# Crossbar transposes for five chunks, a seven-product form of the second MLP product for four chunks, and two groups of zero products, in an attention and Fourier-mixing kernel

## The chip, the cores and the metric

One core of a Trainium2 chip runs the program. The metric is the device time in microseconds of one execution; less is better. The profile is of one execution, and its span runs from the first to the last instruction.

TensorE (PE) multiplies a stationary block with a moving one and writes to PSUM; VectorE (DVE), ScalarE (ACT) and GpSimd (POOL) work on elements; SyncE (SP) issues most transfers. Each engine takes its instructions in the order of its own queue and waits for others by semaphores.

## The reference

```python
# attention with a bias by distance; a key is kept if it is among the first 8,
# or at most 95 places before the query
scores = scale * q @ k.T + bias            # B=4, H=8, S=768, D=64
x = softmax(where(keep, scores, -1e9)) @ v # then heads side by side: B x 768 x 512

# Fourier mixing and a two-layer MLP
mixed = real(fft(fft(x, axis=1), axis=2))
u = x + mixed
un = (u - mean(u)) / sqrt(var(u) + 1e-6)
out = u + relu(un @ w_ch1) @ w_ch2         # w_ch1: 512 x 2048, w_ch2: 2048 x 512
```

## The kernel before

The work falls into four batches. For each one the kernel makes scores, exponentials and the product with V (unit `av`), normalises (`norm`, L699 and L700) into `x`, writes it to DRAM and reads it back in another order of rows (`bounce`), and folds it by additions and subtractions on VectorE (`fold_3`, `fold_s`, `fold_d`). Two stages of small products then make the Fourier transform: `y_unit` (py, L881) and `u_unit` (pu, L961); `mirror` copies reversed blocks on POOL between them.

The MLP takes each batch in three chunks of 256 rows, so there are chunks 0 to 11; chunk 3b + pr belongs to batch b. A chunk consists of two blocks t = 0, 1 of 128 rows. `u_unit` adds the input to the transform (L980), takes the mean away and scales (`un`, L995 on ACT, L997 on DVE). `nt_unit` transposes `un` by eight products with the identity (ptu, L1025) and copies the result out of PSUM to `unT` (L1033 on ACT or L1035 on DVE). The squares for the variance (L1004) overwrite `un`, so they come after the transposes.

The first MLP product of a chunk, `ph_unit` (ph, L1053), has eight units of eight products that are 256 wide; ACT (L1059) or DVE (L1060) applies the maximum with zero and writes `hT`, of which there are three buffers. The second, `pg_unit` (pg, L1076), has four units of four products for each t, 512 wide, all summed in one PSUM bank; L1085 multiplies with the reciprocal deviation and adds to `u`, and a store to the output follows (L1090). The rings `ph` and `pg` have two banks each; `u` has four buffers, `un` and `unT` two.

No loop sets the order. A class `Plan` holds a modelled clock for each engine and, while the program is written, always emits next what can start first in that model. There are four streams for PE: MIX and ATT, in which one of the first ten units can be chosen, and PH and PG, which stay in order. Work for the other engines is announced with `pl.later(ways, needs, after, outs, uses, ...)`: engine and modelled time, what must be there, what it makes, which buffers it frees. Among such operations that could start at the same modelled time, the lower `rank` goes first, then the one that was ready first, then the one announced first. The modelled times decide the order of the queues only; on the chip the semaphores decide.

Of batches 2 and 3 the q and k blocks are already transposed by transfers (`trans_dma`, L494). `expst` holds the exponentials, `mk` the masks that batches 2 and 3 multiply with (L587), `EG` the exponentials of the first eight keys; `EG` is zero at the start, and twelve products with it (L1116) open PE's queue. `v_place` (pvp, L427) puts V of batches 0 and 1 in place by products.

Of the kernel before, what the change touches and what calls it, by code (L numbers as in the profile page):

```python
# [12 lines left out]
ALU = mybir.AluOpType  # L13
# [142 lines left out]
def mm_us(n, k=1):  # L156
    return k * max(n / 2400.0 + 0.0025, 0.029)
# [6 lines left out]
def dve(n):  # L164
    return 0.085 + n / 960.0


def dve2(n):
    return 0.075 + n / 1920.0
# [7 lines left out]
def kernel(  # L177
# [106 lines left out]
    def free(tag, i):  # L284
        i -= NBUF[tag]
        return [("free", tag, i)] if i >= 0 else []

    def buf(tag, i, shape, dtype, users):
        pl.users(("free", tag, i), users)
        return wk.tile(shape, dtype, tag=tag, name=f"{tag}_{i}", bufs=NBUF[tag])  # L290
# [16 lines left out]
    kG = [kon.tile([P, HP, 32], FP16, tag=f"kG{i}", name=f"kG{i}") for i in range(2)]  # L307
    vG = [kon.tile([P, H, 66], FP16, tag=f"vG{i}", name=f"vG{i}") for i in range(2)]

    MIX, ATT, PH, PG = [], [], [], []  # L310
    V = nc.vector
    VT = nc.vector.tensor_tensor
# [105 lines left out]
    def v_place(b, hp):  # L418
        n = HP * b + hp

        def run(start, ring):
            pv = bank(ring, f"pvp_{n}")
            for x in range(NP):
                for a in range(2):
                    for t in range(2):
                        r = slice(64 * a, 64 * a + 64)
                        nc.tensor.matmul(pv[64 * t:64 * t + 64, a, x * P:(x + 1) * P], idn[r, r],  # L427
                                         V0[n][r, x, t].rearrange("p h d -> p (h d)"), start=True, stop=True,
                                         tile_position=(64 * a, 64 * t))
            e = pl.pe(mm_us(P, 12), start)  # L430
            pl.used(("free", "er", n), e)
            done = []

            def freed(t):
                done.append(t)
                if len(done) == 2:
                    pl.rings[ring].append(max(done))
                    for x in CD(b, ring):
                        pl.used(x, max(done))
            for a in range(2):  # L440
                dst = v16[b][:, a::2, 2 * hp:2 * hp + 2, 0:Dh]
                src = pv[:, a, 0:3 * P].rearrange("p (n h d) -> p n h d", h=2, d=Dh)
                ways = [("DVE", dve(384), lambda dst=dst, src=src: V.tensor_copy(dst, src)),
                        ("ACT", act(384), lambda dst=dst, src=src: A(dst, src, AF.Copy))]
                pl.later(ways[a:a + 1],
                         [], e, [("v", b, hp, a)], rank=RA(b), then=freed)
        ATT.append(([("vc", n), ("c", "id")], BANKS(b), run))
# [169 lines left out]
                         e, [("vG", b, half)], (CD(b, ring) if last else ()), ring=ring if last else None, rank=RA(b))  # L617
        ATT.append((VN(b, [2 * half + i for half in halves for i in range(2)]) + [("one", 0)], BANKS(b), run))

    EG = kon.tile([P, 512], FP16, tag="eg", name="eg")  # L620

    def glob(b, halves):

# [326 lines left out]
    def u_unit(b, pr):  # L950
# [62 lines left out]
            pl.later([("POOL", 1.0, rstd)], [("ss", c, 0), ("ss", c, 1)], 0.0, [("rstd", c)], rank=2)  # L1013
        MIX.append((needs + [("c", "t2")], BANKS(b), run))

    def nt_unit(b, pr):
        c = NP * b + pr

        def run(start, ring):
            pt = bank("xx", f"ptu_{c}", FP16)  # L1020
# [22 lines left out]
    def ph_unit(c, jp):  # L1043
        needs = [("unT", c), ("w1", jp // 2)] + (free("hT", 5 + c) if jp == 0 else []) + [("CD",)]

        def run(start, ring):
            if jp == 0:
                HT[c] = buf("hT", 5 + c, [P, NJ, CH], FP16, 2)
            ph = bank("ph", f"ph_{c}_{jp}")
            for a in range(2):  # L1050
                jb = 2 * jp + a
# [14 lines left out]
    def pg_unit(c, t, part):  # L1066
# [4 lines left out]
        def run(start, ring):  # L1071
# [18 lines left out]
                nc.sync.dma_start(out[b].rearrange("(m r) d -> m r d", r=6)[:, rs, :], UT[c][:, t, :])  # L1090
            pl.later([("SP", 0.45, st)], [("ob", i)], 0.0, [], [("free", "u", 2 * HP + c)], lat=1.6, dma=0.7)
        PG.append((needs, ("pg",) if part == 0 else None, run))


    def dma_const(dst, src, us, tok, needs=()):
# [2 lines left out]
    with tc.manual_schedule():  # L1098
# [151 lines left out]
        for c in range(NP * B):  # L1250
            for jp in range(NJ // 2):
                ph_unit(c, jp)
            for t in range(2):
                for part in range(4):
                    pg_unit(c, t, part)
        pl.run([(MIX, True), (ATT, True), (PH, False), (PG, False)])


# [33 lines left out]
```

## Time and profile before

| | us |
|---|---|
| median of 14 runs | 278.48 |
| lowest, highest | 277.04, 280.16 |
| profiled execution | 279.05 |
| its span | 277.3 |
| busy in the span: PE, weight loads, DVE, ACT, POOL | 260.0, 174.3, 157.6, 147.3, 59.7 |

The clock of PE was granted in full except in the slices around 50 us. What is busy where, in 40 equal slices (tenths of a slice):

```profile
PE   8698899589789999999999999999999999999994
PEld 3344548549667864677586566777866677767441
DVE  4565854974785515665378968666896662111121
ACT  1485585584766643797772138888242256434000
POOL 1445195730002502413110031401001320100000
PEclk9999999899999999999999999999999999999999
```

Each slice is 6.9 us long. A busy share is no limit by itself; the last instructions and what they waited for are read from the chain and the timeline, below.

Where the chunks stand on PE's timeline, counting 64 products of ph and 32 of pg for each:

| chunk | transposes (ptu) | first product (ph) begins |
|---|---|---|
| 7 | 172.43 | 183.0 |
| 8 | 176.07 | 195.7 |
| 9 | 221.47 | 224.1 |
| 10 | 223.65 | 234.1 |
| 11 | 230.19 | 246.3 |

The last product of chunk 11's ph ends at 256; after it the pg products of chunks 9 (second half), 10 and 11 follow.

### The profile page before, as it was taken

The numbers are of one execution on the slowest core, as the hardware profiler recorded it, in microseconds if no ns is written. First come the engines' busy times: TensorE is split into PE (matmuls) and PEld (weight loads), VectorE is DVE, ScalarE is ACT, GpSimd is POOL, SyncE is SP. The second block draws the span as 40 slices with busy tenths as digits, with TensorE's granted clock in tenths as the row PEclk, the third lists the DMA queues.
The fourth block names the chain that finished last, engine by engine and source line by source line (L and its number), as shares of the span: only waits on it lengthen the run. The fifth ranks groups of instructions, "written<-read, shape, count | busy, mean of one in ns | idle before, by whom it ended". The sixth has DMA issues, their size and how long they took to land.

```text
span 277.3 us, 6029 instructions
## 1 busy us (share of the span) xinstructions
PE 260.0 (94%) x2460; PEld 174.3 (63%) x2460; DVE 157.6 (57%) x323; ACT 147.3 (53%) x255; POOL 59.7 (22%) x127
## 2 busy tenths in 40 slices
PE   8698899589789999999999999999999999999994
PEld 3344548549667864677586566777866677767441
DVE  4565854974785515665378968666896662111121
ACT  1485585584766643797772138888242256434000
POOL 1445195730002502413110031401001320100000
PEclk9999999899999999999999999999999999999999
DMA  7999999995935597986987896300163020110122
GB/s 206 291 292 286 356 279 230 205 203 105 256 118 168 117 160 167 219 152 132 216 163 166 155 297 130 69 2 0 40 157 150 0 78 1 40 38 27 51 76 76
DMA packets 70301, 40.69 MB, mean 147 GB/s; under 512 B 27394, under 2 KB 66306, under 8 KB 70274
## 3 DMA queue, kind: packets, MB, share of 16 engines
q1 hardware_dynamic: 61474, 29.83, 44.2%
q0 software_dynamic: 4224, 4.19, 9.3%
q10 hardware_dynamic: 4576, 6.29, 8.3%
q8 instruction: 19, 0.31, 0.5%
q14 instruction: 8, 0.07, 0.1%
HBM read 31.92 MB, written 9.44 MB: 149 GB/s over the span
## 4 chain that ended last, share of the span: by engine, by line
PE 77%; DVE 7%; SPq 5%; ACT 3%; DMA 3%; issue 2%; POOL 1%; ACTq 1%; DVEq 0%; POOLq 0%
PE pg L1076 29%; PE ph L1053 29%; PE py L881 5%; SPq L365 4%; PE pav L680 3%; PE sc L552 3%; PE pu L961 3%; DMA w<-in_q_dram 3%; PE ptu L1025 2%; ACT ex L575 1%; PE pav L669 1%; DVE sm L984 1%; DVE qkT L521 1%; POOL ww L929 1%; SPq L1096 1%
## 5 line engine op out<-in xcount | busy, mean ns | idle before, releaser
L1053 PE MATMUL ph<-unT,w 128*128 128x256 f16 x768 | 93.8, 273 | 2.2 <-DVE hT L1060 2.2
L1076 PE MATMUL pg<-w,hT 128*128 128x512 f16 x384 | 89.9, 379 | 0.0
L1053 PEld LDWEIGHTS <-w 128*128 128x128 f16 x768 | 72.6, 98 | 18.4 <-issue 6.1
L1059 ACT ACTIVATE hT<-ph 128x512 f16<-128x512 f32 x73 | 43.6, 597 | 47.6 <-PE ph L1053 46.5
L1076 PEld LDWEIGHTS <-hT 128*128 128x128 f16 x384 | 36.9, 98 | 36.3 <-issue 0.4
L1085 DVE SCALAR_TENSOR_TENSOR u<-pg,sm,u 128x512 f32<-128x512 f32 x24 | 18.0, 749 | 53.6 <-PE pg L1076 53.3
L575 ACT ACTIVATE ex<-sc 128x992 f16<-128x992 f32 (+2 forms) x24 | 20.9, 927 | 13.9 <-PE sc L552 10.1
L1060 DVE TENSOR_SCALAR hT<-ph 128x512 f16<-128x512 f32 x23 | 15.9, 690 | 11.7 <-PE ph L1053 11.6
L572 ACT ACTIVATE er<-sc 128x992 f16<-128x992 f32 (+2 forms) x24 | 21.5, 923 | 1.1 <-PE sc L552 1.1
L369 ACT ACTIVATE qk<-qs 128x384 f16<-128x384 f32 (+1 forms) x31 | 14.5, 528 | 9.9 <-DMA qkT<-qk 7.6
L1011 POOL TENSOR_SCALAR sm<-sm 128x2 f32<-128x2 f32 x12 | 3.1, 262 | 71.6 <-ACT un L1004 71.4
L980 DVE SCALAR_TENSOR_TENSOR u<-pu,xr 128x512 f32<-128x512 f32 x24 | 15.6, 687 | 4.5 <-PE pu L961 3.9
L680 PE MATMUL pav<-v,ex 128*128 128x65 f16 x352 | 16.7, 195 | 1.3 <-ACT ex L575 1.3
L552 PE MATMUL sc<-qkT 64*128 64x256 f16 (+1 forms) x192 | 16.9, 264 | 0.6 <-DVE qkT L521 0.6
L929 POOL COPY ww<-zy 128x512 f16<-128x512 f16 x16 | 9.3, 611 | 37.9 <-PE py L881 37.9
L587 DVE TENSOR_TENSOR ex<-er,mk 128x992 f16<-128x992 f16 (+2 forms) x24 | 14.8, 626 | 4.6 <-ACT er L572 4.4
L680 PEld LDWEIGHTS <-ex 128*128 128x128 f16 x352 | 15.5, 99 | 2.6 <-issue 1.9
L995 ACT ACTIVATE un<-u,sm 128x512 f16<-128x512 f32 x12 | 8.5, 716 | 15.9 <-DVE sm L984 12.9
L1004 ACT ACTIVATE un<-un 128x512 f16<-128x512 f16 x24 | 14.8, 620 | 1.6 <-PE ptu L1025 1.6
L552 PEld LDWEIGHTS <-qkT 64*128 64x128 f16 x192 | 5.9, 94 | 14.7 <-issue 12.2
L898 DVE CAST zy<-py 128x512 f16<-128x512 f32 (+1 forms) x9 | 8.3, 926 | 10.5 <-ACT zy L896 6.4
L896 ACT ACTIVATE zy<-py 128x512 f16<-128x512 f32 (+1 forms) x10 | 8.1, 809 | 11.7 <-PE py L881 11.6
(103 smaller groups left out, 307.4 us busy)
## 6 DMA issues: line engine op xcount, KB each, us to landing
out_dram<-u SPq DMA_DIRECT2D x24, 256.0 KB, 2.3
w<-in_moe_w_ch_dram POOLq DMA_DIRECT2D x8, 512.0 KB, 12.6
qs<-in_q_dram SPq DMA_DIRECT2D x9, 384.0 KB, 5.1
qs<-in_k_dram SPq DMA_DIRECT2D x9, 384.0 KB, 5.9
u<-in_v_dram SPq DMA_DIRECT2D x8, 384.0 KB, 7.3
xr<-xd ACTq DMA_DIRECT2D x4, 768.0 KB, 4.6
qs<-in_v_dram SPq DMA_DIRECT2D x16, 192.0 KB, 4.2
w<-in_q_dram SPq DMA_DIRECT2D x4, 384.0 KB, 6.8
```

Of the source, the lines that this page charges most:

```text
L552: nc.tensor.matmul(pa[:, s, c0:c0 + cw], TT[n][lo:lo + 64, 1, i * P:(i + 1) * P], TT[n][lo:lo + 64, 0, i * P:i * P + cw], start=(b > 1), s ...
L572: A(mine(), cut(pa), AF.Exp, 0.0, 0.125)
L575: A(cut(expst[hp][:, :, g * 512:g * 512 + (384 if g == 2 else 512)]), cut(pa), AF.Exp, 0.0, 0.125)
L587: VT(o, mine(), m, op=ALU.mult)
L680: nc.tensor.matmul(po[:, jj, hh * 65:(hh + 1) * 65], lhsT, v16[b % 2][:, i, h, 0:65], start=(jp == 0 and a == 0), stop=(a == len(ops) - 1) ...
L980: V.scalar_tensor_tensor(u[:, a].rearrange("p (n r) -> p n r", r=4), pu[:, a].rearrange("p (r n) -> p n r", r=4), 1.0, XR[b][:, rr].rearra ...
L1004: A(x, x, AF.Square, accum_out=MV[c][:, a, 2:3])
L1053: nc.tensor.matmul(ph[:, a * CH:(a + 1) * CH], W1[0][:, d, jb * P:(jb + 1) * P], UNT[c][:, d, :], start=(d == 0), stop=(d == ND - 1))
L1059: pl.later([("ACT", act(512), lambda: A(dst, ph, AF.Relu)), ("DVE", dve(512), lambda: V.tensor_scalar_max(dst, ph, 0.0))], [], e, [("h", c ...
L1060: ("DVE", dve(512), lambda: V.tensor_scalar_max(dst, ph, 0.0))],
L1076: nc.tensor.matmul(pg, HT[c][:, jb, t * P:(t + 1) * P], W2[0][:, jb, :], start=(jb == 0), stop=(jb == NJ - 1))
L1085: V.scalar_tensor_tensor(UT[c][:, t, :], pg, MV[c][:, t, 3:4], UT[c][:, t, :], op0=ALU.mult, op1=ALU.add)
```

## The change

It has three parts.

- Chunks 7 to 11: `nt_dma` takes the place of the PE transposes. Two transfers on SP's queue, one for each t, write `unT` directly.
- Chunks 8 to 11: the second product is made from seven block products. `hT` is a matrix of 2 x 2 blocks (t by halves of the 2048), `w_ch2` one of 2 x 2 blocks (halves of the 2048 by halves of the 512 columns). `w2_sums` makes four sums of blocks of `w_ch2`, once, and keeps them in `expst`; `s_sums` makes four sums of blocks of `hT` for each chunk, three in `mk`, one in place. `pg_units` multiplies: seven products of eight matmuls, 256 wide, in five units (`p1`, `p45`, `p6`, `p32`, `p7`) with two PSUM banks, A and D. After each unit one addition to `u` follows, five in all. Bank A is summed into further: the left block of u(0) takes it after `p1`, the right block after `p6`, and both blocks of u(1) take it after `p7`; bank D goes to both blocks of u(1) after `p45`, and, partly summed further, to both of u(0) after `p32`.
- In `v_place` of batch 0 ten products of zeros stand before the second placement (n = 1) and fourteen after the first (n = 0). They write a part of the bank that nothing reads. `EG` is allocated earlier for them.

```diff
--- before.py
+++ after.py
@@ -307,6 +307,7 @@
     kG = [kon.tile([P, HP, 32], FP16, tag=f"kG{i}", name=f"kG{i}") for i in range(2)]
     vG = [kon.tile([P, H, 66], FP16, tag=f"vG{i}", name=f"vG{i}") for i in range(2)]
 
+    EG = kon.tile([P, 512], FP16, tag="eg", name="eg")
     MIX, ATT, PH, PG = [], [], [], []
     V = nc.vector
     VT = nc.vector.tensor_tensor
@@ -420,6 +421,9 @@
 
         def run(start, ring):
             pv = bank(ring, f"pvp_{n}")
+            idle = lambda k: [nc.tensor.matmul(pv[:, 1, 3 * P:4 * P], EG[:, 0:P], EG[:, 0:P], start=True, stop=True) for _ in range(k)]
+            if n == 1:
+                idle(10)
             for x in range(NP):
                 for a in range(2):
                     for t in range(2):
@@ -427,6 +431,8 @@
                         nc.tensor.matmul(pv[64 * t:64 * t + 64, a, x * P:(x + 1) * P], idn[r, r],
                                          V0[n][r, x, t].rearrange("p h d -> p (h d)"), start=True, stop=True,
                                          tile_position=(64 * a, 64 * t))
+            if n == 0:
+                idle(14)
             e = pl.pe(mm_us(P, 12), start)
             pl.used(("free", "er", n), e)
             done = []
@@ -617,7 +623,6 @@
                          e, [("vG", b, half)], (CD(b, ring) if last else ()), ring=ring if last else None, rank=RA(b))
         ATT.append((VN(b, [2 * half + i for half in halves for i in range(2)]) + [("one", 0)], BANKS(b), run))
 
-    EG = kon.tile([P, 512], FP16, tag="eg", name="eg")
 
     def glob(b, halves):
 
@@ -1013,8 +1018,19 @@
             pl.later([("POOL", 1.0, rstd)], [("ss", c, 0), ("ss", c, 1)], 0.0, [("rstd", c)], rank=2)
         MIX.append((needs + [("c", "t2")], BANKS(b), run))
 
+    def nt_dma(c):
+        for a in range(2):
+            def xb(a=a):
+                if a == 0:
+                    UNT[c] = buf("unT", c, [P, ND, CH], FP16, 1)
+                nc.sync.dma_start_transpose(UNT[c][:, :, a * P:(a + 1) * P], T[("un", c)][:, a])
+            pl.later([("SP", 1.3, xb)], [("un", c, a)] + (free("unT", c) if a == 0 else [("nx", c, 0)]), 0.0, [("nx", c, a)], lat=0.0, dma=0.01)
+        pl.later([("SP", 0.0, lambda: None)], [("nx", c, 1)], 0.0, [("unT", c)], [("free", "un", c)], lat=2.2, dma=0.3)
+
     def nt_unit(b, pr):
         c = NP * b + pr
+        if c >= 7:
+            return nt_dma(c)
 
         def run(start, ring):
             pt = bank("xx", f"ptu_{c}", FP16)
@@ -1045,7 +1061,7 @@
 
         def run(start, ring):
             if jp == 0:
-                HT[c] = buf("hT", 5 + c, [P, NJ, CH], FP16, 2)
+                HT[c] = buf("hT", 5 + c, [P, NJ, CH], FP16, 2 if c < CS else 1)
             ph = bank("ph", f"ph_{c}_{jp}")
             for a in range(2):
                 jb = 2 * jp + a
@@ -1090,6 +1106,146 @@
                 nc.sync.dma_start(out[b].rearrange("(m r) d -> m r d", r=6)[:, rs, :], UT[c][:, t, :])
             pl.later([("SP", 0.45, st)], [("ob", i)], 0.0, [], [("free", "u", 2 * HP + c)], lat=1.6, dma=0.7)
         PG.append((needs, ("pg",) if part == 0 else None, run))
+
+
+    NK = NJ // 2
+    HC = Dm // 2
+    CS = 8
+    SX = {}
+
+    def W2T(i):
+        return expst[i].rearrange("p s n -> p (s n)")[:, 0:NK * HC].rearrange("p (k n) -> p k n", n=HC)
+
+    def w2_sums(i):
+
+        def run():
+            k0 = slice(4 * i, 4 * i + 4)
+            k1 = slice(NK + 4 * i, NK + 4 * i + 4)
+            w = W2[0]
+            b11, b12 = w[:, k0, 0:HC], w[:, k0, HC:Dm]
+            b21, b22 = w[:, k1, 0:HC], w[:, k1, HC:Dm]
+            VT(W2T(1)[:, k0], b22, b12, op=ALU.subtract)
+            VT(W2T(3)[:, k0], b12, b11, op=ALU.subtract)
+            VT(W2T(0)[:, k0], b22, W2T(3)[:, k0], op=ALU.subtract)
+            VT(W2T(2)[:, k0], b21, W2T(0)[:, k0], op=ALU.subtract)
+        pl.later([("DVE", 4 * dve2(1024), run)], [("avdone", B - 1), ("w2", 3)] + [("ex", B - 1, hp, g) for hp in range(HP) for g in range(3)], 0.0, [("w2t", i)], rank=2)
+
+    def s_sums(c):
+        hs = [("h", c, jp) for jp in range(NJ // 2)]
+
+        def block(t, half):
+            return HT[c][:, half * NK:(half + 1) * NK, t * P:(t + 1) * P]
+
+        def new(i):
+            k = 3 * (c - CS) + i
+            pl.users(("free", "sx", k), 2 if i < 2 else 1)
+            SX[c, i] = mk.rearrange("p h n -> p (h n)")[:, (k % 4) * NK * P:(k % 4 + 1) * NK * P].rearrange("p (k n) -> p k n", n=P)
+            return SX[c, i]
+
+        def s1():
+            VT(new(0), block(1, 0), block(1, 1), op=ALU.add)
+
+        def s3():
+            VT(block(1, 0), block(0, 0), block(1, 0), op=ALU.subtract)
+
+        def s2():
+            VT(new(1), SX[c, 0], block(0, 0), op=ALU.subtract)
+
+        def s4():
+            VT(new(2), block(0, 1), SX[c, 1], op=ALU.subtract)
+        us = dve2(NK * P)
+
+        def sfree(i):
+            k = 3 * (c - CS) + i - 4
+            return [("free", "sx", k)] if k >= 0 else []
+        pl.later([("DVE", us, s1)], hs + sfree(0), 0.0, [("s", c, 1)], rank=1)
+        pl.later([("DVE", us, s2)], [("s", c, 1)] + sfree(1), 0.0, [("s", c, 2)], [("free", "sx", 3 * (c - CS))], rank=1)
+        pl.later([("DVE", us, s4)], [("s", c, 2)] + sfree(2), 0.0, [("s", c, 4)], [("free", "sx", 3 * (c - CS) + 1)], rank=1)
+        pl.later([("DVE", us, s3)], [("s", c, 1)], 0.0, [("s", c, 3)], rank=1)
+
+    def pg_units(c):
+        b, pr = divmod(c, NP)
+        rs = PAIRS[pr]
+        t1s, t2s, t3s, t4s = 0, 0, 1, 2
+
+        def prod(o, lhs, rhs, first, last=True):
+            for j in range(NK):
+                nc.tensor.matmul(o, lhs(j), rhs(j), start=(first and j == 0), stop=(j == NK - 1), skip_group_check=True)
+
+        def a(t, half):
+            return lambda j: HT[c][:, half * NK + j, t * P:(t + 1) * P]
+
+        def sx(i):
+            return lambda j: SX[c, i][:, j, :]
+
+        def bw(half, col):
+            return lambda j: W2[0][:, half * NK + j, col * HC:(col + 1) * HC]
+
+        def tw(i):
+            return lambda j: W2T(i)[:, j, :]
+        u = lambda t: UT[c][:, t, :]
+        r = lambda t: MV[c][:, t, 3:4]
+        one_us = mm_us(HC, NK)
+
+        def stt(o, x, t, acc):
+            V.scalar_tensor_tensor(o, x, r(t), acc, op0=ALU.mult, op1=ALU.add)
+
+        def p1(start, ring):
+            A_ = GP[c, "A"] = bank("pg", f"pgA_{c}")
+            prod(A_[:, 0:HC], a(0, 0), bw(0, 0), True)
+            e = pl.pe(one_us, start)
+            pl.later([("DVE", dve(HC), lambda: stt(u(0)[:, 0:HC], A_[:, 0:HC], 0, u(0)[:, 0:HC]))],
+                     [("rstd", c)], e, [("ra", c, 0)], rank=0)
+
+        def p45(start, ring):
+            D_ = GP[c, "D"] = bank("pg", f"pgD_{c}")
+            prod(D_[:, 0:HC], a(1, 1), tw(2), True)
+            prod(D_[:, HC:Dm], sx(0), tw(3), True)
+            e = pl.pe(2 * one_us, start)
+            pl.used(("free", "sx", 3 * (c - CS)), e)
+            pl.later([("DVE", dve(Dm), lambda: stt(u(1), D_, 1, u(1)))],
+                     [("rstd", c)], e, [("rd", c, 0)], rank=0)
+
+        def p6(start, ring):
+            A_ = GP[c, "A"]
+            prod(A_[:, 0:HC], sx(1), tw(0), False)
+            e = pl.pe(one_us, start)
+            pl.used(("free", "sx", 3 * (c - CS) + 1), e)
+            pl.later([("DVE", dve(HC), lambda: stt(u(0)[:, HC:Dm], A_[:, 0:HC], 0, u(0)[:, HC:Dm]))],
+                     [], e, [("ra", c, 1)], rank=0)
+
+        def p32(start, ring):
+            D_ = GP[c, "D"]
+            prod(D_[:, HC:Dm], sx(2), bw(1, 1), False)
+            prod(D_[:, 0:HC], a(0, 1), bw(1, 0), True)
+            e = pl.pe(2 * one_us, start)
+            pl.used(("free", "sx", 3 * (c - CS) + 2), e)
+            pl.later([("DVE", dve(Dm), lambda: stt(u(0), D_, 0, u(0)))],
+                     [("ra", c, 1)], e, [("ob", c, 0)], ring="pg", rank=0)
+
+        def p7(start, ring):
+            A_ = GP[c, "A"]
+            prod(A_[:, 0:HC], a(1, 0), tw(1), False)
+            e = pl.pe(one_us, start)
+            pl.used(("free", "hT", 5 + c), e)
+
+            def last():
+                o = u(1).rearrange("p (x n) -> p x n", x=2)
+                stt(o, A_[:, 0:HC].unsqueeze(1).to_broadcast([P, 2, HC]), 1, o)
+            pl.later([("DVE", dve(Dm), last)], [("rd", c, 0)], e, [("ob", c, 1)], ring="pg", rank=0)
+
+        h0 = [("h", c, jp) for jp in range(4)]
+        h1 = [("h", c, jp) for jp in range(4, 8)]
+        ws = [("w2t", 0), ("w2t", 1)]
+        PG.append((h0 + ws, ("pg",), p1))
+        PG.append((h1 + [("s", c, 1)], ("pg",), p45))
+        PG.append(([("s", c, 2), ("ra", c, 0)], None, p6))
+        PG.append(([("s", c, 4), ("rd", c, 0)], None, p32))
+        PG.append(([("s", c, 3), ("ra", c, 1)], None, p7))
+        for t in range(2):
+            def st(t=t):
+                nc.sync.dma_start(out[b].rearrange("(m r) d -> m r d", r=6)[:, rs[t], :], u(t))
+            pl.later([("SP", 0.45, st)], [("ob", c, t)], 0.0, [], [("free", "u", 2 * HP + c)], lat=1.6, dma=0.7)
 
 
     def dma_const(dst, src, us, tok, needs=()):
@@ -1250,9 +1406,15 @@
         for c in range(NP * B):
             for jp in range(NJ // 2):
                 ph_unit(c, jp)
+            if c >= CS:
+                s_sums(c)
+                pg_units(c)
+                continue
             for t in range(2):
                 for part in range(4):
                     pg_unit(c, t, part)
+        for i in range(2):
+            w2_sums(i)
         pl.run([(MIX, True), (ATT, True), (PH, False), (PG, False)])
 
 
```

## The prediction

> **What bounds the kernel now.** I read the page first (span, slices, chain, groups), then the busy time in stages, then the timeline of TensorE and VectorE around the places that the change touches. The profiled run took 279.05 us; its span is 277.3 us, so 1.75 us lie around it. The median of the 14 runs is 278.48 us, 0.57 below the profiled one. I sum against 279.05 and take 0.57 off at the end.
>
> The chain of waits says what carries the end:
>
> ```profile
> PE 77%; DVE 7%; SPq 5%; ACT 3%; DMA 3%; issue 2%; POOL 1%; ACTq 1%; DVEq 0%; POOLq 0%
> ```
>
> The reader is to see that TensorE (PE) alone is three quarters of it. By stage:
>
> ```profile
> 98.00:133.00 35.00, 35.00 (x286) 23.18 (x285) 17.73 (x34) 22.39 (x44) 8.15 (x20) 1.00 0.87 165
> 133.00:182.00 49.00, 49.00 (x459) 31.87 (x456) 35.60 (x72) 28.30 (x51) 8.27 (x21) 1.00 0.75 166
> 182.00:199.00 17.00, 17.00 (x222) 13.21 (x219) 12.16 (x24) 12.10 (x20) 0.88 (x2) 1.00 0.05 17
> 199.00:214.00 15.00, 15.00 (x107) 10.22 (x105) 12.50 (x25) 5.45 (x8) 0.10 (x1) 1.00 0.45 126
> 214.00:231.00 17.00, 17.00 (x155) 12.00 (x154) 10.24 (x24) 7.17 (x16) 4.73 (x11) 1.00 0.12 46
> 231.00:256.00 25.00, 25.00 (x192) 18.54 (x190) 3.63 (x5) 11.37 (x21) 0.88 (x2) 1.00 0.06 22
> 256.00:273.40 17.40, 17.29 (x81) 7.63 (x78) 3.00 (x5) 0.60 (x1) 0.00 (x0) 1.00 0.20 75
> ```
>
> The columns are window, length, then busy time of PE, weight loads, DVE (VectorE), ACT, POOL, the clock, DMA. From 98 us on PE is never without work; the others are, most of all at the end. A matmul's end is modelled, so the busy time alone would prove little; I confirm it by starts: on the timeline 80 products of L1076 begin at 255.86 and end 17.43 us later, 216 ns each, with nothing between.
>
> **Prices.** From the groups split by form:
>
> ```profile
> L1076 PE MATMUL pg<-w,hT 128*128 128x512 f16 x384 | 89.9, 379 | 0.0
> L1085 DVE SCALAR_TENSOR_TENSOR u<-pg,sm,u 128x512 f32<-128x512 f32 x24 | 18.0, 749 | 53.6 <-PE pg L1076 53.3
> L1025 PE MATMUL ptu<-ident,un 128*128 128x128 f16 x96 | 7.3, 219 | 2.5 <-ACT un L995 2.5
> L1035 DVE COPY unT<-ptu 128x1024 f16<-128x1024 f16 x9 | 6.2, 689 | 8.8 <-PE ph L1053 6.1 <-PE ptu L1025 2.7
> L750 DVE TENSOR_TENSOR ww<-eA 128x1024 f16<-128x1024 f16 x3 | 2.1, 692 | 0.3
> ```
>
> The 219 and 379 ns are latencies that overlap; what counts is start to start. On the chain eight ptu transposes take 0.45 us (56 ns each), sixteen ph products of width 256 take 1.75 us (109 ns), four pg products of width 512 take 0.86 us (216 ns). The Trainium skill, "TensorE: Matmul & The Clock Gate", section "Back-to-back issue gap", gives N/2.4 + 2.5 ns for a single stream, which is 109 and 216 ns here; the same section claims other gaps (131 ns at N=512) for load-and-multiply streams, and this trace contradicts those. So a product cut to width 256 costs its half, and its own weight load (98 ns) stays hidden, as it does in ph.
>
> **What the skill says of the rest.** "DMA: Bandwidth & Descriptors", section "DMA Transpose (X-bar)", says that the crossbar takes two-byte data from SP or ACT, which fits; "Advanced Engine Details and Errata", section "X-Bar Transpose (TRN2)", expects 350 to 400 GB/s. A transfer here is 128 KB, so an estimate from that page is about 0.35 us of moving. The trace shows that the fixed part is larger: 32 transposes of 96 KB took 1.25 us each on SP's queue and 2.4 to 8.8, median 3.7 us, to land, under load. "VectorE: DVE Perf Modes", section "What auto-detection actually checks", gives a two-tensor operation on 16-bit data twice the base rate; L750 at 0.69 us for 1024 elements agrees, and it is the price for each new sum.
>
> **The change, part by part.**
>
> *Transposes.* Five chunks lose 8 PE transposes each: 5 x 0.45 = 2.25 us of PE, all after 171 us where PE is full. Their copies (0.69 on DVE or 1.02 on ACT) go too. Added are ten transfers on SP, 2 x 1.25 us and a landing for each chunk, about 5 us after `un`, against 1.2 us (transposes and copy) before. SP's queue holds q and k transposes until 176 and later only output stores; a store behind a transfer that waits for `un` goes out late, which matters for the `u` buffer of chunk 11 alone. Chunks 7 and 8 are ready at 172 and 176 and are first used at 183.0 and 195.7, by counting 64 ph products a chunk, so they are covered. Chunk 9 is the first doubtful one.
>
> *Seven products.* One chunk's second product is now 32 x 216 ns = 6.91 us; then 56 x 109 = 6.12. Four chunks save 3.15 us. Together with the transposes PE loses 5.4 us of work.
>
> *VectorE's added work.* Eight weight sums (5.5 us) once; four sums a chunk (2.75 us, four times, 11 us); five result additions instead of two: three of 0.75 and two of 256 elements, which I put at 0.48, so 3.2 us against 1.5. In 199 to 231 us DVE is busy 22.7 of 32 us. Added there: 5.5 + 2.75 + at most 3.2 for chunk 8, minus 1.4 for two copies. That is 32.8 of 32 us: DVE has nothing left in this stretch.
>
> Where it bites is the order. The weight sums become ready with `avdone` of the last batch, at the same planned time and with the same rank 2 as the last normalisation of that batch; they were registered earlier, so they stand ahead of it in DVE's queue:
>
> ```profile
> 199.19 0.20 DVE L699 RECIPROCAL rc<-pav 128x8 f32<-128x8 f32 x1
> 199.42 0.69 DVE L700 TENSOR_TENSOR x<-pav,rc 128x512 f16<-128x512 f32 x1
> 200.14 0.96 DVE L744 TENSOR_TENSOR eA<-x 128x1536 f16<-128x1536 f16 x1
> ```
>
> Behind that normalisation wait the last batch's fold, its y, mirror, u and `un`, thus chunk 9. So I expect this chain 5.5 us later, and about another 2.75 when chunk 8's sums slip into the gaps of the fold; 0.9 comes back since PE reaches 199 sooner. In before, `un` of chunk 9 is ready at 217.84 (its last piece on ACT). Then 217.84 + 5.5 + 2.75 - 0.9 = 225.2, and two transfers with landing, 4 to 5 us, give 229.2 to 230.2.
>
> What covers this on PE:
>
> ```profile
> 221.47 0.61 PE L1025 MATMUL ptu<-ident,un 128*128 128x128 f16 x8
> 221.92 1.89 PE L1076 MATMUL pg<-w,hT 128*128 128x512 f16 x8
> 223.65 0.61 PE L1025 MATMUL ptu<-ident,un 128*128 128x128 f16 x8
> 224.09 1.91 PE L1053 MATMUL ph<-unT,w 128*128 128x256 f16 x16
> ```
>
> Chunk 9's first product begins at 224.1. Without four groups of transposes that place comes at 222.3, and the 6.1 us of chunk 8's second product can be drawn ahead: PE has work until 228.4. So PE idles 0.8 to 1.8 us in this estimate; below, nothing, if DVE's gaps (1.3 and 0.8 us near 212 and 213) absorb part of the shift; above, 5.4, if all DVE additions fall in front of chunk 9. I take 0.8. With chunk 8 used up, chunk 9's first products run without others between and wait on two PSUM banks: 0.3 us.
>
> *The tail.* After chunk 11's first product PE has 1.5 to 2 chunks of block products. The fourth unit waits for the addition of the D bank: 0.75 plus some 0.25 of latencies, against 0.87 of product between; the same holds at two bank changes. That is 3 x 0.15 = 0.45 us a chunk if DVE is free. DVE has chunk 11's sums there as well (0.69 each, in order), so I take 1.1 us in all, between 0.5 and 2. The very end, an addition and a store, keeps its 3.9 us.
>
> *Products of zeros.* 14 x 56 ns = 0.78 us after the first V placement and 10 x 56 = 0.56 before the second. PE stands idle there for 0.84 us (from 10.4) and 0.78 us (to 13.3), waiting for ACT and POOL, so they fit; if that cover were gone they would cost 1.3. The clock was granted in full at that time and fell to half only within 49 to 56 us, which they don't reach. I take 0, between -0.5 and +0.6.
>
> **Sum.** 279.05 - 5.4 + 0.8 + 0.3 + 1.1 = 275.85; less 0.57, 275.3 us.
>
> **Rivals.**
>
> *All hidden.* DVE's shift stays inside PE's stock of work and only the smallest tail stall remains: -5.4 + 0.5, so 273.6. For it: PE's stock reaches to 228.4. Against: 32.8 us of DVE work for 32.
>
> *The gain is spent.* VectorE sets the pace from 199 us to the end; the wait ahead of chunk 9 reaches 2.5 and the tail's stalls 2: 278.48 - 5.4 + 2.5 + 0.3 + 2 = 277.9. For it: DVE, in the last 12 us, has nearly as much work as PE (5.95 us against 6.1 for each chunk). Against: sums of chunk 10 can be made during chunk 11's first product, where DVE was nearly idle.
>
> *Slower.* One mechanism: the weight sums in front of the last normalisation, with every later sum and addition of chunk 8 ahead of chunk 9. The chain is then 11.4 us late, chunk 9 lands at 217.84 + 11.4 - 0.9 + 4.5 = 232.8 and PE idles 4.4 us; the tail's 2 and 0.3 come on top, and a PE order planned for earlier arrivals makes it idle some 1.5 to 2 more as the in-order units wait for sums: 278.48 - 5.4 + 4.4 + 2.3 + 1.8 = 281.6. It ends slower from a wait ahead of chunk 9 of about 4 us on.
>
> That the change doesn't do what it says is no rival of weight: both the shorter list of products and the missing transposes are explicit.
>
> **How the numbers follow.** Forecast (274.3 to 277.3) 0.56; all hidden (272.8 to 274.3) 0.18; spent 0.13; slower 0.13. A change of 0.3% (0.84 us) is about what a measurement of this kernel can tell from none: faster is below 277.6, slower above 279.3. The first two cases and a part of the third are faster: 0.76; same 0.11; slower 0.13. The range from 272.8 to 278.4 leaves out the slower case and little else.
>
> **What would show it.** Right: 56 products of width 256 a chunk at 109 ns and PE's list shorter by 5.4 us; DVE with eight sums ahead of the last normalisation; chunk 9's first product near 229 with a PE wait of a microsecond before it; short waits on DVE in the last 12 us. Wrong: block products slower than 109 ns; transfers landing much later than 3 us; a PE wait of over 3 us after 199, or none at all; or a shift before 170 us, where I expect none.

## The result and the profile after

| | us |
|---|---|
| changed kernel, median of 10 runs | 274.26 (273.03 to 275.90) |
| kernel before, beside it, median of 48 runs | 278.84 |
| ratio, 95% interval | 0.9835 [0.9813, 0.9857] |
| profiled execution's span, before and after | 277.3, 272.7 |

The change saves 4.6 us. The forecast was 275.3 us, 1.0 more than was measured. The nature of the bound has not changed; this is the line of the chain of waits by engine, after:

```profile
PE 75%; DVE 8%; SPq 7%; ACT 3%; issue 2%; DMA 2%; POOL 1%; ACTq 0%; DVEq 0%; POOLq 0%
```

TensorE still carries it. In stages (window, length, then the busy time of PE, weight loads, DVE, ACT, POOL, the clock, DMA share, GB/s):

```profile
171.00:199.00 28.00, 28.00 (x313) 20.18 (x312) 20.80 (x40) 22.25 (x39) 3.83 (x8) 1.00 0.22 49
199.00:214.00 15.00, 15.00 (x101) 9.61 (x100) 14.23 (x27) 5.58 (x9) 0.00 (x0) 1.00 0.49 141
214.00:231.00 17.00, 16.82 (x158) 13.28 (x157) 11.10 (x27) 6.81 (x14) 4.41 (x11) 1.00 0.26 63
231.00:256.00 25.00, 25.00 (x231) 22.41 (x230) 11.25 (x18) 10.17 (x19) 1.30 (x3) 1.00 0.21 54
256.00:269.00 13.00, 12.72 (x114) 10.88 (x112) 6.96 (x13) 2.39 (x4) 0.00 (x0) 1.00 0.11 42
```

DVE is the engine that took on work: 14.23 of 15 us between 199 and 214, and 6.96 of 13 at the end, where it was almost idle before. PE stays full but for 0.18 us between 214 and 231 and 0.28 us in the last window, 0.1 of which lies behind its last product.

A busy PE proves little, so I compare starts: the transposes of chunk 6 and PE's last products, before and then after.

```profile
171.12 0.61 PE L1025 MATMUL ptu<-ident,un 128*128 128x128 f16 x8
...
255.86 17.43 PE L1076 MATMUL pg<-w,hT 128*128 128x512 f16 x80
```

```profile
170.96 0.61 PE L1041 MATMUL ptu<-ident,un 128*128 128x128 f16 x8
...
267.86 1.04 PE L1173 MATMUL pgA<-ex,hT 128*128 128x256 f16 x8
```

From the transposes of chunk 6 to the end of PE's last product (273.29, 268.90) there are 102.17 and 97.94 us: 4.23 saved where the list of work is shorter by 5.4. So 1.17 of the 5.4 were given back. 0.2 lies behind the last product (4.0 us to the end of the span before, 3.8 after).

This stretch repeats closely. It is 97.94 us again in a second profile of the changed kernel, 97.95 in that of the change without the zeros, and 102.17 in that of the kernel with the zeros alone. The time ahead of it does not repeat: chunk 6's transposes begin between 169.15 and 171.18 us in the thirteen profiles that have them on PE, and at 170.96 and 169.68 in the two of the changed kernel. So the 0.16 us by which the change is ahead at that place tell nothing, and below I compare traces from there on.

This timeline of PE after shows most of what was given back (start, length, line, operation, idle time and its releaser):

```profile
222.51 1.04 PE L1173 MATMUL pgA<-w,hT 128*128 128x256 f16 x8
223.73 1.03 PE L1173 MATMUL pgD<-ex,hT 128*128 128x256 f16 x8 [0.18 <-DVE u L1101]
...
225.47 1.91 PE L1069 MATMUL ph<-unT,w 128*128 128x256 f16 x16
227.22 1.04 PE L1173 MATMUL pgA<-ex,mk 128*128 128x256 f16 x8
...
261.28 1.04 PE L1173 MATMUL pgA<-ex,hT 128*128 128x256 f16 x8
262.49 1.03 PE L1173 MATMUL pgA<-w,hT 128*128 128x256 f16 x8 [0.18 <-DVE u L1191]
...
265.11 1.04 PE L1173 MATMUL pgA<-ex,mk 128*128 128x256 f16 x8
266.11 1.03 PE L1173 MATMUL pgD<-w,mk 128*128 128x256 f16 x8
```

Eight block products take 0.87 us from start to start (109 ns each) where nothing waits. From 222.51 to 223.73 they take 0.35 more, from 261.28 0.34, from 265.11 0.13: 0.82 us of waits. By the profile the first two are for PSUM banks that DVE's additions had not yet released; the third, too short to have a releaser there, is at a change of banks too. The line at 225.47 is chunk 9's first product: it begins without a wait.

The remaining 0.35 fits a cost that no view names, and that no run tested by itself. In the changed order, ten blocks of score products (64 rows) stand between the 128-row products after 171 us where there were eight; PE after:

```profile
173.91 1.05 PE L1069 MATMUL ph<-unT,w 128*128 128x256 f16 x8
174.89 0.39 PE L558 MATMUL sc<-qkT 64*128 64x256 f16 x4
175.21 1.05 PE L1069 MATMUL ph<-unT,w 128*128 128x256 f16 x8
```

Here eight ph products take 0.98 instead of 0.87 from start to start and four score products 0.32, where eight in one block take 0.47 to 0.53. Four more switches at about 0.1 us are 0.4; summed over all blocks, the score products and the delay just ahead of them take 0.44 us more than before.

The prices of DVE's new work, from the groups split by form (count, then busy us and mean ns, then idle time ahead and its releaser):

```profile
L1191 DVE SCALAR_TENSOR_TENSOR u<-pgD,sm,u 128x512 f32<-128x512 f32 x8 | 6.0, 749 | 11.3 <-PE pgD L1173 11.3
...
L1191 DVE SCALAR_TENSOR_TENSOR u<-pgA,sm,u 128x256 f32<-128x256 f32 x8 | 3.8, 481 | 2.2 <-PE pgA L1173 2.1
...
L1146 DVE TENSOR_TENSOR mk<-hT 128x1024 f16<-128x1024 f16 x4 | 2.8, 690 | 5.1 <-ACT hT L1075 5.1
```

0.69 for a sum, 0.48 and 0.75 for the additions: as put in. What the forecast had otherwise is the time at which the last normalisation comes. DVE after:

```profile
194.17 0.68 DVE L1127 TENSOR_TENSOR ex<-w 128x1024 f16<-128x1024 f16 x1
...
198.86 0.69 DVE L1130 TENSOR_TENSOR ex<-w,ex 128x1024 f16<-128x1024 f16 x1
...
199.70 0.69 DVE L705 TENSOR_TENSOR x<-pav,rc 128x512 f16<-128x512 f32 x1
```

The eight weight sums do stand ahead of the normalisation, and yet it starts at 199.70, 0.28 later than before (199.42), not 4.6 later. It also waits for products (pav). The last group of these, before and after:

```profile
198.61 0.41 PE L680 MATMUL pav<-v,ex 128*128 128x65 f16 x8
```

```profile
194.42 0.41 PE L685 MATMUL pav<-v,ex 128*128 128x65 f16 x8
```

They come 4.2 us earlier, or 4.0 counted from chunk 6's transposes (27.49 and 23.46 us behind these). So the sums ran in the time that the earlier products had made free.

### The profile page after: what moved, and what is told of

It reads as the page before. It is cut to its first block, busy times and chain, and to the rows that moved or that the text cites. A ratio compares the mean times of both kernels' runs of the same rounds, so it can differ in the third digit from the quotient of the medians.

```text
span 272.7 us, 6251 instructions
## 1 busy us (share of the span) xinstructions
PE 256.6 (94%) x2540; PEld 183.0 (67%) x2540; DVE 172.8 (63%) x351; ACT 148.7 (55%) x258; POOL 61.4 (23%) x127
## 4 chain that ended last, share of the span: by engine, by line
PE 75%; DVE 8%; SPq 7%; ACT 3%; issue 2%; DMA 2%; POOL 1%; ACTq 0%; DVEq 0%; POOLq 0%
PE ph L1069 29%; PE pg L1092 19%; SPq L366 6%; PE py L886 5%; PE pgD L1173 5%; PE pgA L1173 3%; PE sc L558 3%; PE pav L685 3%; PE pu L966 3%; DMA w<-in_q_dram 2%; PE ptu L1041 1%; ACT ex L581 1%; PE pav L674 1%; DVE qkT L527 1%; DVE u L985 1%
## 5 line engine op out<-in xcount | busy, mean ns | idle before, releaser
L1075 ACT ACTIVATE hT<-ph 128x512 f16<-128x512 f32 x75 | 44.7, 597 | 50.5 <-PE ph L1069 49.5
L1092 PE MATMUL pg<-w,hT 128*128 128x512 f16 x256 | 60.5, 379 | 0.0
L1092 PEld LDWEIGHTS <-hT 128*128 128x128 f16 x256 | 24.3, 98 | 23.9 <-issue 0.8
L1101 DVE SCALAR_TENSOR_TENSOR u<-pg,sm,u 128x512 f32<-128x512 f32 x16 | 12.0, 749 | 20.1 <-PE pg L1092 20.0
L1076 DVE TENSOR_SCALAR hT<-ph 128x512 f16<-128x512 f32 x21 | 14.5, 690 | 9.9 <-PE ph L1069 9.9
L903 DVE CAST zy<-py 128x512 f16<-128x512 f32 (+1 forms) x8 | 7.7, 957 | 11.3 <-ACT zy L901 6.4
```

The lines of the kernel that those rows point to most:

```text
L1075: pl.later([("ACT", act(512), lambda: A(dst, ph, AF.Relu)), ("DVE", dve(512), lambda: V.tensor_scalar_max(dst, ph, 0.0))], [], e, [("h", c ...
L1092: nc.tensor.matmul(pg, HT[c][:, jb, t * P:(t + 1) * P], W2[0][:, jb, :], start=(jb == 0), stop=(jb == NJ - 1))
```

## The experiments

Ratios are against the kernel before, run beside it on the same chip (medians of 278.15 to 278.41 us). The theory after the result was: PE's shorter list is the whole gain, both parts add up, and the last batch moved forward so far that the weight sums fell into a gap. Its main rival: one part carries all, or DVE's new order costs nothing at any place.

**One part alone.** Only the transposes by DMA:

```diff
-            if n == 1:
-                idle(10)
...
-            if n == 0:
-                idle(14)
...
-    CS = 8
+    CS = 12
...
-        for i in range(2):
-            w2_sums(i)
```

> Only the crossbar transposes of chunks 7 to 11; the second product and V's placement as before. If the gain is TensorE's shorter list, this saves 5 x 0.45 = 2.25 us minus at most 0.4 of waits: 276.6 to 277.0 beside a before of 278.8, ratio 0.992 to 0.9935. If instead the transposes matter by an earlier start of the last batch (its scores moved 4 us forward), the saving exceeds 2.25 us: ratio under 0.991. If the transfers' landing is late for chunk 9, TensorE waits before chunk 9 and the ratio is over 0.995.

Measured: 276.78, ratio 0.9943 [0.9931, 0.9955], 1.6 us faster. The ratio lies between those of the forecasts, nearest to that of the shorter list.

Only the seven products:

```diff
-            if n == 1:
-                idle(10)
...
-            if n == 0:
-                idle(14)
...
-        if c >= 7:
-            return nt_dma(c)
```

> Only the seven block products of chunks 8 to 11; transposes on TensorE and no added zeros. If the list is what counts, 3.15 us go and 0.8 come back as tail waits: 276.4 to 276.6, ratio 0.991 to 0.9925. If VectorE's sums hold up the last batch as the prediction had it (here nothing brings the last batch forward), TensorE waits ahead of chunk 9 by 1 us or more and the ratio is 0.995 or over.

Measured: 276.08, ratio 0.9923 [0.9907, 0.994], 2.1 us faster. Both are below the work taken off the list (2.25 and 3.15). In the traces, from chunk 6's transposes to PE's last product, the first takes 100.30 us and the second 99.94: 1.87 and 2.23 saved, 4.10 together, where the change saves 4.23. With the seven products alone the last normalisation ends at 205.48 and chunk 9 begins at 230.23, as late as the forecast had it, yet with a wait of only 0.24 us: PE's own transposes and a copy are a short way from `un`.

Only the products of zeros (both edits above but for the `idle` lines, which stay), and the change without them:

> Only the 24 products of zeros. If they lie in waits of TensorE and the clock is full there anyway: no change, ratio 0.998 to 1.002. If they keep the clock from falling in a part of the executions: ratio 0.994 to 0.997. If they delay the placement of V: up to +1.3 us, ratio 1.003 to 1.005.

Measured: 277.93, ratio 0.9986 [0.9971, 1.0002].

> The changed kernel without the 24 products of zeros. By the shorter list alone the time stays at 274.3 (273.9 to 274.7), ratio to before 0.982 to 0.985. If the zeros carry a part of the gain, 275.2 or more, ratio 0.987 or more.

Measured: 274.18, ratio 0.986 [0.9838, 0.9882], between its two forecasts. The two parts alone give -0.57% and -0.77%, together -1.34%; both without zeros -1.40%. They add up; the rival of one part that carries all falls. The zeros are not told from nothing: the first ratio holds 1, and with and without them the intervals overlap. From chunk 6 on the trace is the same without them (97.95 us), so what they do, if they do anything, lies ahead of that place.

**The weight sums.** Each done twice, same values again, so that DVE has another 5.5 us ahead of the last normalisation:

```diff
-            VT(W2T(1)[:, k0], b22, b12, op=ALU.subtract)
+            for _ in range(2):
+                VT(W2T(1)[:, k0], b22, b12, op=ALU.subtract)
...
```

> The changed kernel with the eight weight sums made twice (the same values written again), so VectorE has 5.5 us more in front of the last batch's last normalisation; TensorE's order is unchanged. If the chain through that normalisation is covered only just, as its distance to chunk 9 (landing near 223.5, first use 225.5, so 2 us) says, TensorE waits 2 to 3.5 us ahead of chunk 9: 276.3 to 277.8, ratio 0.990 to 0.996. If VectorE's idle places absorb it, under 1 us: ratio under 0.987.

Measured: 279.63, ratio 1.0044 [1.0022, 1.0066]: 2.1% above the change (5.8 us), more than expected, and at another place. PE with the sums twice:

```profile
200.71 1.89 PE L1092 MATMUL pg<-w,hT 128*128 128x512 f16 x8
206.80 3.25 PE L1069 MATMUL ph<-unT,w 128*128 128x256 f16 x16 [4.20 <-ACT hT L1075]
```

This is chunk 8's first product, not chunk 9's. ACT in that kernel, and then in the changed one, tells why:

```profile
204.82 1.28 ACTq L724 DMA_DIRECT2D xd<-x  x2
206.15 1.08 ACT L1075 ACTIVATE hT<-ph 128x512 f16<-128x512 f32 x2 [7.25 <-issue]
```

```profile
200.43 1.27 ACTq L724 DMA_DIRECT2D xd<-x  x2
201.75 1.09 ACT L1075 ACTIVATE hT<-ph 128x512 f16<-128x512 f32 x2 [1.94 <-PE ph L1069]
```

The write of `x` to memory is issued from ACT's queue and waits for the last normalisation; chunk 8's maxima stand behind it, and ph has no free bank until they are made. In both kernels the write starts within 0.05 us of the end of the normalisation (204.79 and 200.39), and the maxima follow when it is issued. No run put the write on another queue, so this rests on the traces. In the changed kernel the same passes with PE never idle. The write moved by 4.4 us (200.43 to 204.82) and PE idled 4.2. In the busy time by window of the kernel with the sums twice, the clock then dropped:

```profile
206.80:210.20 3.40, 3.40 (x17) 2.37 (x17) 3.40 (x8) 1.14 (x3) 0.00 (x0) 0.55 0.93 230
```

That is 0.55 of full speed for 3.4 us. The two blocks of products behind the wait take 1.7 us longer from start to start than in the changed kernel, and the wait costs 4.4 from start to start. Together these are the 6.0 us by which the stretch from 200.71 (201.63 in the changed kernel) to the end of PE's last product is longer (73.30 against 67.27); the medians give 5.8. The Trainium skill, "TensorE: Matmul & The Clock Gate", Part 1, section "What's actually happening", describes a clock that is judged in windows of 4096 cycles (3.41 us) and halved after an idle one. This trace agrees in the length: in finer windows the clock is 0.96 from 206.80 to 207.20, 0.50 from there to 210.40 and 1.00 from 210.60 on.

The opposite: the last normalisation ahead of the sums.

```diff
-        pl.later([("DVE", 4 * dve2(1024), run)], [("avdone", B - 1), ("w2", 3)] + [("ex", B - 1, hp, g) for hp in range(HP) for g in range(3)], 0.0, [("w2t", i)], rank=2)
+        pl.later([("DVE", 4 * dve2(1024), run)], [("x", B - 1, hp, jp) for hp in range(HP) for jp in range(NP)] + [("avdone", B - 1), ("w2", 3)] + [("ex", B - 1, hp, g) for hp in range(HP) for g in range(3)], 0.0, [("w2t", i)], rank=2)
```

> The changed kernel with the weight sums held until the last batch is normalised, so the fold's chain starts some 4 us sooner. If the sums ahead of the normalisation cost nothing in the changed kernel because TensorE has other work, the time stays: 273.9 to 274.8, ratio 0.982 to 0.985. If they still cost, up to 1 us less: ratio 0.979 to 0.981. If the sums now come too late for chunk 8's products, TensorE waits and the ratio is over 0.986.

Measured: 273.61, ratio 0.9824 [0.9787, 0.9860]. The normalisation then ends at 195.42, 5.0 us sooner, and the time is that of the change within the interval. From chunk 6's transposes to the last product the trace takes 97.72 us, 0.2 less than the change. So in the change the sums' place costs nothing that the times show, and 0.2 us in the trace, while another 5.5 us costs 6.0 in the trace: 4.4 for the wait, the rest for the clock behind it.

**Which chunks go by DMA.** From chunk 9 on only, so that 7 and 8 are transposed by PE:

```diff
-        if c >= 7:
+        if c >= 9:
```

> The changed kernel with chunks 7 and 8 transposed on TensorE again. If the transfers of chunks 7 and 8 are what moved the last batch's scores 4 us forward, they move back, the last normalisation ends near 205.5 instead of 200.4, and chunk 9's transfers land near 230 while TensorE has work until 229.5: a wait of 0 to 1.5 us besides the 0.9 us of transposes: 275.0 to 276.5, ratio 0.986 to 0.992. If the last batch stays forward, only the 0.9 us come: ratio 0.986 to 0.988 and no wait at chunk 9.

Measured: 275.99, ratio 0.9911 [0.9872, 0.9949]: about 2 us short of the change (1.75 in the trace: 99.69 against 97.94), where the two chunks' transposes are 0.9 us. DVE and PE of this kernel:

```profile
203.78 0.69 DVE L705 TENSOR_TENSOR x<-pav,rc 128x512 f16<-128x512 f32 x1
```

```profile
227.49 1.04 PE L1173 MATMUL pgA<-ex,hT 128*128 128x256 f16 x8
229.36 2.86 PE L1069 MATMUL ph<-unT,w 128*128 128x256 f16 x24 [0.83 <-DMA unT<-un]
```

This is close to the forecast's scene: the normalisation 4.4 us later than before (5.3 counted from chunk 6's transposes, where the sums take 5.5), chunk 9 at 229.36, PE idle 0.83 us for the transfer (1.0 by starts: 1.87 for a unit of 0.87). The last group of pav stands 27.49 us behind chunk 6's transposes, as before. So the transfers of chunks 7 and 8, which I had called merely covered, are what removed it, and PE's shorter list is not the whole of their gain. ACT's timeline, before and after, suggests how:

```profile
172.89 0.62 ACT L1004 ACTIVATE un<-un 128x512 f16<-128x512 f16 x1
...
174.11 0.62 ACT L1004 ACTIVATE un<-un 128x512 f16<-128x512 f16 x1
...
174.73 1.65 ACT L572 ACTIVATE er<-sc 128x960 f16<-128x960 f32 x2
```

```profile
172.52 0.62 ACT L1009 ACTIVATE un<-un 128x512 f16<-128x512 f16 x1
...
173.13 1.76 ACT L578 ACTIVATE er<-sc 128x960 f16<-128x960 f32 x2
```

Squares of `un` wait for `unT`. Where that comes by DMA it comes later, so ACT does one square and goes on to the last batch's exponentials at 173.13; before, three squares stood ahead of them (174.73). PE's order differs as well, since `Plan` emits every queue anew after an edit: the change has four score products at 172.36 and four at 173.64, the kernel with the transfers from 9 has eight at 172.88. To try the squares, the transfers begin at chunk 9 as above and the squares of chunks 7 and 8 are held back until the last exponential product:

```diff
-                         [("unT", c)], 0.0, [("ss", c, a)], [("free", "un", c)], rank=3)
+                         [("unT", c)] + ([("ex", B - 1, HP - 1, 2)] if c in (7, 8) else []), 0.0, [("ss", c, a)], [("free", "un", c)], rank=3)
```

> As the kernel with the transfers from chunk 9 on, but ACT's squares of chunks 7 and 8 are held until the last batch's scores are through. If ACT's work on chunks 7 and 8 (squares) is what kept the last batch's scores back, the last normalisation ends 1.5 us or more before the 204 to 205 that it had, and TensorE's wait of 1 us ahead of chunk 9 is gone: ratio 0.985 to 0.989. If the order of the first product or SP's queue is what matters, nothing moves: ratio 0.989 to 0.993 and the wait stays.

Measured: 274.84, ratio 0.9874 [0.9831, 0.9917]. The interval overlaps that of the kernel without the hold, so the time doesn't decide. DVE, then PE:

```profile
201.54 0.69 DVE L705 TENSOR_TENSOR x<-pav,rc 128x512 f16<-128x512 f32 x1
```

```profile
226.35 1.03 PE L1173 MATMUL pgD<-w,mk 128*128 128x256 f16 x8 [1.06 <-DVE u L1191]
...
228.09 1.91 PE L1069 MATMUL ph<-unT,w 128*128 128x256 f16 x16
```

The normalisation is 2.2 us earlier than without the hold (201.54 against 203.78), but 1.0 of this had come before chunk 6's transposes (169.15 against 170.17), where executions differ anyway. Counted from these transposes the normalisation is 1.2 us earlier and the last group of pav 1.4 (26.10 against 27.49; 23.46 in the change). So holding the squares back brings 1.4 of the 4.0 us by which the change leads there. The two chunks' transposes are another 0.9; the remaining 1.7 (the copies, PE's order) was not taken apart.

The wait ahead of chunk 9 is gone, as forecast for the squares; instead PE waits 1.06 us for a bank just before. From chunk 6's transposes to the last product the trace takes 99.76 us, against 99.69 without the hold, so by itself the hold saved nothing there.

More chunks by DMA, from 3 on:

```diff
-        if c >= 7:
+        if c >= 3:
```

> The changed kernel with the transfers for chunks 3 to 11. If TensorE's list is what counts and its stock of other products covers the landing, 4 x 0.45 = 1.8 us more are saved: 272.3 to 273.0, ratio 0.976 to 0.979. If chunk 3 has too little work ahead of it, or SP's loads stand in the way of the transfers (and the transfers in the way of the loads), the saving is gone: ratio 0.983 or more.

Measured: 280.55, ratio 1.0087 [1.0063, 1.0110]: 2.5% slower than the change, although PE's list is another 1.8 us shorter. Its SP queue and its busy time in one window:

```profile
171.86 1.19 SPq L1026 DMA_TRANSPOSE unT<-un  x1
173.16 2.50 SPq L500 DMA_TRANSPOSE qkT<-qk  x2
```

```profile
167.00:184.00 17.00, 11.62 (x116) 7.60 (x113) 12.00 (x29) 12.58 (x18) 4.37 (x11) 0.75 0.57 111
```

PE is busy 11.62 of 17 us, at 0.75 of the clock; the changed kernel has 17.00 there at 1.00. Chunk 6's transfers share SP's queue with the q and k transposes (two more of `un` follow at 175.75), and its first product starts at 180.75, against 173.91 in the change. The queue is what I read from the trace; it was not taken apart from the lack of other work for PE at that time.

**The change again, and two banks more.** The change unedited, beside the others:

> The changed kernel once more, beside the three that follow on the same chip: 273.9 to 274.8, ratio 0.982 to 0.985.

Measured: 273.46, ratio 0.9819 [0.9783, 0.9855].

Then the normalisation first, as above, with bank A of chunks 10 and 11 from the bank of the transposes, which stands free there:

```diff
-            A_ = GP[c, "A"] = bank("pg", f"pgA_{c}")
+            A_ = GP[c, "A"] = bank("xx", f"pgA_{c}")[:, 0, :] if c >= 10 else bank("pg", f"pgA_{c}")
...
-        PG.append((h0 + ws, ("pg",), p1))
+        PG.append((h0 + ws, ("xx",) if c >= 10 else ("pg",), p1))
```

(and the release of that bank in p7 accordingly).

> The changed kernel with the weight sums behind the last normalisation, and bank A of chunks 10 and 11 taken from the two-bank ring that the Fourier stage no longer needs. If the tail's waits come from the two banks, 0.3 to 0.8 us of the 0.8 us go: 273.2 to 274.0, ratio 0.980 to 0.983, and in the profile no wait of pgA after 250. If VectorE's sums are what the tail waits for, the waits stay and so does the time.

Measured: 272.99, ratio 0.9808 [0.9770, 0.9846]; its PE in the tail:

```profile
259.53 1.04 PE L1173 MATMUL pgA<-ex,hT 128*128 128x256 f16 x8
260.41 1.04 PE L1173 MATMUL pgA<-w,hT 128*128 128x256 f16 x8
```

0.88 us from one to the next: the wait at the bank change is gone, and the stretch from chunk 6's transposes is 97.38 us, against 97.72 with the normalisation first alone. That bank alone, without the zeros:

> The changed kernel with that bank for chunks 10 and 11 and without the 24 products of zeros. If the zeros do nothing: the same as the one before it or as the changed kernel, 273.4 to 274.6, ratio 0.980 to 0.985. If they save some tenths by holding the clock up, 0.5 to 1 us more than the changed kernel in the same call.

Measured: 273.99, ratio 0.9834 [0.9789, 0.9879]. The three intervals overlap. In the trace the stretch is 97.61 us, against 97.94 in the change: the bank takes away its wait of about 0.34 us both times. A faster kernel than the change is not shown by the times.

## Why the prediction was right, and where its sum was off

The two savings and all prices held, and the time fell within the range. It lies at the border between the forecast (from 274.3 us) and the rival "all hidden" (up to 274.3), and what happened on PE is nearer to that rival: no wait ahead of chunk 9, and a small tail. Of the prediction's own signs, "chunk 9's first product near 229 with a PE wait of a microsecond before it" did not come (225.47, no wait), and of a PE wait after 199 only 0.35 us came ahead of the tail, close to the "none at all" among its signs of being wrong. The rival's reason was not right either: the shift was not absorbed by PE's stock of work, most of it did not take place.

- *Transposes, 2.25 us, and products, 3.15 us.* Right. Block products took 109 ns. Alone, the transposes brought 1.6 us and the products 2.1, less than their list in both: each has its own losses.
- *VectorE's added work.* Right in each price and in the order (eight sums ahead of the last normalisation). The 32.8 of 32 us between 199 and 231 were not reached: DVE was busy 25.3, since the eight sums ran before 199.5.
- *The wait ahead of chunk 9, 0.8 us.* This is the term that failed: it measured 0, the lower bound given. The step that failed is "0.9 comes back since PE reaches 199 sooner". What came back was 4.2: the last pav group began at 194.42 instead of 198.61. I had counted PE's saved transposes only, and not that the last batch's scores could move forward. Squares out of ACT's way are worth 1.4 us of it, by the run that held them back; 1.7 stays open. So the normalisation came 0.28 us later instead of 4.6, and chunk 9's `un` was ready at 219.83, 2.0 later than before instead of 7.4. Its transfers had landed by 223.73, when ACT's squares of it begin, and PE had other work until 225.47. With chunks 7 and 8 left on PE, the wait stood where it was put, 0.83 us at 229.36.
- *Chunk 9 on two banks, 0.3.* Measured 0: chunk 8's block products still alternate with chunk 9's first product (225.47 and 227.22 above). In the kernel with the transfers from chunk 9 on, which had used chunk 8 up, such a wait came: 0.26 us at 232.48.
- *The tail, 1.1 us.* Measured 0.47 (0.34 + 0.13), just under the lower bound of 0.5; it comes at two bank changes, not as 0.15 at each. Another 0.35 fell on the bank change inside chunk 8 behind 222.51, where none was put.
- *Switches between shapes.* Not in the sum; the 0.35 that is left, or 0.4 by the count of switches.
- *Zeros, 0.* Not told from 0: alone they lie between 0.8 us faster and 0.1 slower.
- *No shift before 170 us.* None is shown: 0.16 us, where two executions of the changed kernel differ by 1.3.
- *Sum.* 0.8 + 0.3 + 1.1 = 2.2 was taken off the 5.4; 1.17 was measured. The three terms were 1.7 too large, and 0.7 that no term had (chunk 8's bank, the switches) made up for a part, which is luck. In the two profiles 0.36 came from outside that stretch, 0.16 of it by chance. So the saving was 4.6 us instead of 3.2. The kernel before measured 0.4 above the median that the forecast started from, which leaves the 1.0 between 275.3 and 274.26.
- *The rival "slower".* Its direction can happen: with 5.5 us more on DVE the kernel was slower than before. But its place was wrong. The first to be late is not chunk 9 through the fold and the transfers, but chunk 8's maxima, behind a DMA on ACT's queue. Nothing in the forecast named what stands behind that DMA.

## What to carry to other kernels

When work is put ahead of a step on an in-order engine, ask first when that step's input will be ready in the new order; a change elsewhere may have moved it by more than the added work. Taking work off can be worth more than its own time, if what stands next in the queues feeds the late chain: chunks 7 and 8 by transfer took 0.9 us off PE's list and, in the traces, 1.75 off its time. And list what stands behind every DMA issued from a compute engine's queue: it waits with it.

## What the runs showed of the hardware

- Going from 128-row to 64-row products and back costs about 0.1 us each time (eight ph products 0.98 instead of 0.87 us; four score products 0.32, where eight take 0.47 to 0.53).
- A transfer of `un` through the crossbar (10 of them) held SP's queue for 1.21 us in the median, and landed 2.4 to 4.1 us after its issue, median 2.5; q and k, under load, had taken 3.7.
- With the clock at 1.00 from there on, PE's stretch of about 100 us from chunk 6's transposes to the last product repeated within 0.01 us between executions (97.94 twice in the changed kernel, 97.95 without the zeros; 102.17 in the kernel before, with and without them), while the 170 us ahead of it varied by 2 over all kernels.
- The time of an execution goes with its mean clock. Of the kernel before, beside the kernel with the sums twice, ten executions at 0.998 or more took 277.4 us in the median, twelve at 0.985 or 0.988 took 279.4.
- Whether the clock falls to half in the idle stretch near 50 us varies between profiled executions, with the same idle time there. These are the windows from 46 to 58 us of the change without zeros, then of the transposes alone:

```profile
46.00:58.00 12.00, 8.94 (x152) 5.79 (x151) 10.52 (x21) 8.29 (x16) 9.20 (x17) 1.00 1.22 200
```

```profile
46.00:58.00 12.00, 9.20 (x118) 6.22 (x115) 9.88 (x20) 6.60 (x13) 8.79 (x17) 0.72 1.23 203
```

The clock is 1.00 and 0.72, that is no and two halved windows of 3.41 us; the kernel before had one (0.86), and so had the change. In the kernel before and in the two shown, PE's idle stretch is the same 2.49 us, waiting for ACT's `un`. The section of the skill cited above speaks of an idle window of about 3.4 us; here less was enough in two of three. It also calls the window free-running. That would fit, if what counts is how the stretch falls on the window, but three executions don't show it. A comparison of two single profiles can be off by this.
